# One row transfer an iteration from a ring, ranks in a rotating PSUM bank, and a reordered start

## The chip, the cores and the metric

The kernel runs on one NeuronCore of one Trainium2 chip. The core has four compute engines that run side by side, each through its own list of instructions in order: TensorE (PE in the profile; weight loads are PEld), VectorE (DVE), ScalarE (ACT) and GpSimd (POOL). SyncE (SP) only starts transfers. Transfers that SP starts and those that GpSimd starts use different queues on the same 16 DMA engines. The metric is the device time in microseconds (us) of one execution. The engines wait for each other through semaphores, which a framework places wherever one instruction needs what another leaves; the order within each engine is the order of the program text.

## The reference

Attention with a local window, then a dense MLP plus a mixture of eight experts with one expert a token:

```
B, H, S, D = 4, 8, 768, 64        # 3072 tokens, model width 512
for each chunk of 32 queries:
    keys, values = 8 memory rows + 16 left + 32 own + 8 right     # 64 rows
    a = softmax(q @ keys.T / 8);  attn = a @ values
x = attn as [3072, 512]
y = relu(x @ w1_dense) @ w2_dense
logits = x @ w_gate;  e = argmax;  gate = softmax(logits)[e]
y += gate * (relu(x @ w1[e]) @ w2[e])
```

All inputs and the output are float32; the large products run in bfloat16, the products that decide the gate in float32.

## The kernel before

There are two stages. The first goes over 24 tiles of 128 tokens (six a batch) and ends by scattering each tile's rows into a buffer `xs` in device memory, sorted by expert. The second fetches 31 slots of 128 rows from `xs`, multiplies each by its expert's weights and scatters the result to the output.

A row that is scattered has 770 words (`ROW`): x in bfloat16, the dense result in float32 (from `YD`), the gate weight (`GW`) and the token number (`GW + 1`). Rows are made in groups (`GROUPS`): seven groups of three tiles, then one of two and one of one. A group's rows lie in one tile `row` of a pool with two buffers.

**The loop (L481 to L532).** Iteration g works on several tiles at once: scores of tile g, the turning of the probabilities of g - 1, `values` of g - 2, `turn_x` of g - 3, and gate, dense1, dense2 of g - 4. There are 28 iterations. The program text gives each engine its order: gate and dense1, `turn_x`, scores, values, one key or query block of the next batch (`turn_qk`), turn, exp, dense2, perhaps another block, rank, ship.

- `values` (L278) leaves the attention output `xn` (one buffer). GpSimd casts it into `row` (L297).
- `turn_x` (L300) transposes `xn`; ScalarE copies it to `x32`, then VectorE casts it to `xT`, in this order.
- `gate` (L310) writes logits into the PSUM tile `pgt`. With the last tile of a group it calls `choose` (L357), which finds the expert and leaves `ex`, `oh`.
- `rank` (L383) counts, for a group, how many earlier tokens chose the same expert. Its matmuls write another part of the same tile `pgt`; VectorE reads it at L404 and leaves the row numbers `si` (L409). It also sums `ex` and writes the gate weights into the rows (L401, L402).
- `ship` (L413) starts the group's three scatters on GpSimd, one after the other (L416).
- `new_group` (L350) takes the next `row` buffer and copies the token numbers into it (L355).

PSUM tiles named `ps` rotate over three buffers: `xtp`, `sc`, `tp`, `ap` take them in turn, and each taker waits until the one three before has been read.

**Values.** The values of half a batch lie in one of three tiles `vw`: 64 rows a head, of which 8 are memory rows. `fill_v` (L154) writes the memory rows from `memv` over a whole block, `load_v` and `load_end` (L161, L179) then load the values over it, and `shift_v` (L189) copies the rows that two neighbouring chunks share. In the loop the fills run on GpSimd in every iteration with g % 3 = 1, and the shifts on VectorE and ScalarE in those with g % 3 = 0 and 1. A load of expert weights by GpSimd (L83) follows the ship from iteration 6 on.

**The start (L448 to L478).** Four pairs of key and query loads are started on GpSimd, then the first values, the memories and the gate weights on SP; VectorE clears both key tiles `kbd` and fills its half of `vw` 0; the memory keys `mk` follow the four pairs; ScalarE fills the other half. Then come constants, two more pairs, the dense weights, the fill of `vw` 1 on GpSimd, and the transposes of batch 0: eight steps through the `ps` buffers, emptied by ScalarE and VectorE (L224, L230). The key copies on VectorE wait for those on ScalarE.

GpSimd's transfers use eight semaphores in turn, and so do SP's: each transfer waits until the eighth before it has landed.

Of the kernel before, what the change touches and what calls it, by code (L numbers as in the profile page):

```python
# [38 lines left out]
GRP = 3  # L39
# [7 lines left out]
def kernel(  # L47
# [63 lines left out]
    with ExitStack() as one:  # L111
# [4 lines left out]
        rows = one.enter_context(tc.tile_pool(name="rows", bufs=2))  # L116
# [12 lines left out]
        memv = c1.tile([128, B * HP, D], F32, name="memv")  # L129
        wgate = c1.tile([128, DT, E], F32, name="wgate")  # L130
        mk = c1.tile([128, 128], BF16, name="mk")

        qk_todo = [(b, hp) for b in range(B) for hp in range(HP)]
        qk = {}
# [102 lines left out]
        def attention(g, qT, kbd):  # L237
# [40 lines left out]
            def values():  # L278
                vw = vws[g // 3 % NV]
                xp = px.tile([128, 2, 512], F32, tag="xp", name="xp")  # L280
                for hp in range(HP):
                    for par in range(2):
                        r = slice(64 * par, 64 * par + 64)
                        for cc in range(4):
                            nc.tensor.matmul(  # L285
                                xp[32 * cc:32 * cc + 32, par, (D + 1) * hp:(D + 1) * (hp + 1)],
                                st["aT"][r, hp, 32 * cc:32 * cc + 32],
                                vw[r, hp, 4 * (g % 3) + cc, :], start=True, stop=True,
                                tile_position=(64 * par, 32 * cc))
                xv = xp[:, :, :HP * (D + 1)].rearrange("p a (h d) -> p a h d", d=D + 1)  # L290
                rs = small.tile([128, 2, HP], F32, tag="rs", name="rs")
                nc.vector.reciprocal(rs, xv[:, :, :, D])
                xn = work.tile([128, DM], F32, tag="xn", name="xn")
                nc.vector.tensor_tensor(  # L294
                    xn.rearrange("p (h a d) -> p a h d", a=2, d=D), xv[:, :, :, :D],
                    rs.unsqueeze(3).to_broadcast([128, 2, HP, D]), ALU.mult)
                nc.gpsimd.tensor_copy(grp["row"][:, u, :YD].bitcast(BF16), xn)  # L297
                st["xn"] = xn

            def turn_x():  # L300
# [8 lines left out]

            def gate():  # L310
                for d in range(DT):
                    nc.tensor.matmul(grp["pg"][:, 0, u, :], st["x32"][:, d, :], wgate[:, d, :],  # L312
                                     start=(d == 0), stop=(d == DT - 1))
                if u == grp["size"] - 1:
                    choose(grp)
# [18 lines left out]
            def last(part):  # L334
                if u == grp["size"] - 1:
                    part(grp)

            return {"scores": scores, "exp": expo, "turn": turn, "values": values,
                    "turn_x": turn_x, "gate": gate, "dense1": dense1, "dense2": dense2,
                    "rank": lambda: last(rank), "ship": lambda: last(ship)}  # L340
# [7 lines left out]
        pgt = pg.tile([128, 3, 2, GRP, E], F32, name="pgt")  # L348

        def new_group(n):  # L350
            grp = grps[n]
            grp["row"] = rows.tile([128, GRP, ROW], F32, tag="row", name="row")
            grp["pg"] = pgt[:, n % 2]
            k, t = grp["size"], grp["first"]
            nc.gpsimd.tensor_copy(grp["row"][:, :k, GW + 1].bitcast(I32), tok[:, t:t + k])  # L355

        def choose(grp):  # L357
            k = grp["size"]
            SH = [128, k, E]

            def wide(ap):
                return ap.unsqueeze(2).to_broadcast(SH)

            def st(shape, name, dt=F32):
                return small.tile(shape, dt, tag=f"{name}{k}", name=name)

            lg = grp["pg"][:, 0, :k]
# [12 lines left out]
            nc.scalar.activation(ex, df, AF.Exp, bias=0.0, scale=1.0)  # L380
            grp["ex"], grp["oh"] = ex, oh

        def rank(grp):  # L383
            k = grp["size"]
            SH = [128, k, E]
            rk, row, ex, oh = grp["pg"][:, 1, :k], grp["row"], grp["ex"], grp["oh"]

            def st(shape, name, dt=F32):
                return small.tile(shape, dt, tag=f"{name}{k}", name=name)


# [8 lines left out]
            es = st([128, k], "es")  # L400
            nc.vector.reduce_sum(es, ex, axis=AX.X)  # L401
            nc.vector.reciprocal(row[:, :k, GW], es)  # L402
            at = st(SH, "at")
            nc.vector.tensor_tensor(at, rk, ecap.unsqueeze(1).to_broadcast(SH), ALU.add)  # L404
            nc.vector.tensor_tensor(at, at, oh, ALU.mult)
            sl = st([128, k], "sl")
            nc.vector.reduce_sum(sl, at, axis=AX.X)
            si = st([128, k], "si", I32)
            nc.vector.tensor_copy(si, sl)  # L409
            nc.vector.tensor_tensor(oh_sum[:, :k], oh_sum[:, :k], oh, ALU.add)  # L410
            grp["si"] = si

        def ship(grp):  # L413
            row, si = grp["row"], grp["si"]
            for t in range(grp["size"]):
                i = nc.gpsimd.indirect_dma_start(  # L416
                    xs[:, :], bass.IndirectOffsetOnAxis(ap=si[:, t:t + 1], axis=0),
                    row[:, t, :].bitcast(I32), None, bounds_check=E * SPAN - 1, oob_is_err=False)
                for o in scatters:
                    tc.declare_no_dep(i.ins, o.ins, reason="different rows of xs")  # L420
                scatters.append(i)


        thr_i = c1.tile([128, NT], I32, name="thr_i")
# [20 lines left out]
                nc.vector.memset(low[:, e, :e], 1.0)  # L445


        for _ in range(HP):  # L448
            load_qk()
        nc.vector.memset(memv, 0.0)  # L450
        for vw in vws:
            nc.vector.memset(vw[:, :, :, D:], 1.0)
        for par in range(2):
            nc.vector.memset(vws[0][64 * par:64 * par + 32, :, 0, :D], 0.0)
        load_v(0)
        load_memories()
        nc.sync.dma_start(wgate, moe_w_gate.rearrange("(t p) m -> p t m", p=128))
        for kb in kbds:
            nc.vector.memset(kb, 0.0)
        nc.vector.memset(mkbd, 0.0)  # L460
        load_mk()
        for par in range(2):
            fill_v(0, nc.scalar.copy if par else nc.vector.tensor_copy,
                   slice(64 * par + 32, 64 * par + 64))
        load_end(0)
        constants()
        table_constants()
        for _ in range(QKB - HP):
# [8 lines left out]
            s()  # L477
        mem_keys()  # L478
        steps = []
        ALL = slice(0, HP)  # L480
        for g in range(NT + 4):  # L481
            def do(part, lag):
                if 0 <= g - lag < NT:
# [51 lines left out]
        def tmp(shape, name, dt=F32):  # L535
            return small.tile(shape, dt, name=name, bufs=1)

        cp = pgt[:, 2, 0, 0]
# [185 lines left out]
```

## Time and profile before

| | us |
|---|---|
| median of the runs (309.37 to 314.36) | 309.46 |
| profiled execution | 309.23 |
| its span, first to last instruction | 307.5 |
| first scores on TensorE | 27.09 |
| last scatter to `xs` starts | 219.33 |
| first fetch of `xs` ends TensorE's wait | 227.83 |
| last output scatter starts | 299.52 |

TensorE is busy for 75% of the span, VectorE 62%, ScalarE 50%, GpSimd 45%; the mean granted TensorE clock is 0.904 of full speed. The DMA engines moved 54.1 MB.

The profile is read in this way. The chain of work that ended last goes back from the last instruction to whatever released each one. The table of waits adds up, for each line, how long its engine stood idle before it and which instruction ended that. A timeline lists instructions as "start, duration, engine, line, operation, output <- input", with the idle time before in brackets. A table of stretches gives the busy time of each engine (instructions in brackets), then the granted clock, the DMA share and GB/s. "Issue" is idle time for which the profile shows no cause.

### The profile page before, as it was taken

To read this page: it belongs to the slowest core of one execution; us is meant where nothing else is said; L and a number is where in the kernel's file an instruction comes from. 1 tells how busy PE (TensorE), PEld (TensorE's weight loads), DVE (VectorE), ACT (ScalarE), POOL (GpSimd) and SP (SyncE) were. 2 spreads that over 40 slices of the span, in tenths; PEclk is the share of its full clock that TensorE was granted. 3 is DMA by queue.
4 is the path that set the end of the run, shared out by engine and by line. 5 is a ranking of instruction groups with operands and counts; after the bars stand their busy time and mean duration, and the time that the engine had idled before them with its cause. 6 is when DMAs were issued, how large, how long until landed. Compare 5 with 4: busy or idle time off the path is not lost.

```text
span 307.5 us, 9871 instructions
## 1 busy us (share of the span) xinstructions
PE 231.3 (75%) x4028; PEld 182.3 (59%) x4063; DVE 190.8 (62%) x424; ACT 154.0 (50%) x240; POOL 138.8 (45%) x160
## 2 busy tenths in 40 slices
PE   0216788968888877978878788969229869999990
PEld 0115577756766765866766667858127547766760
DVE  6356666767768767768874744634824547776760
ACT  0085766755575664766754454523105435555540
POOL 9187634437457227327335032042202625556552
PEclk9999989997997997989986976995857999999996
DMA  7979999658999959957968915340373999998830
GB/s 125 186 98 181 191 205 131 110 129 167 187 192 212 156 95 206 166 122 179 179 124 176 272 63 205 104 156 13 143 230 112 233 344 306 320 317 294 288 117 0
DMA packets 56076, 54.10 MB, mean 176 GB/s; under 512 B 30558, under 2 KB 47966, under 8 KB 56032
## 3 DMA queue, kind: packets, MB, share of 16 engines
q0 software_dynamic: 22896, 31.53, 49.4%
q1 hardware_dynamic: 33136, 21.95, 29.9%
q8 instruction: 32, 0.52, 0.7%
q14 instruction: 12, 0.10, 0.1%
HBM read 50.31 MB, written 20.74 MB: 231 GB/s over the span
## 4 chain that ended last, share of the span: by engine, by line
PE 38%; issue 22%; POOL 12%; DVE 10%; ACT 6%; POOLq 1%; DVEq 0%; ACTq 0%
POOL out_dram L668 11%; PE xp L285 8%; PE ph L321 7%; PE pgt L312 7%; PE py L330 5%; PE ap L273 3%; PE xtp L303 3%; PE tp L219 3%; DVE vw L193 2%; PE sc L252 2%; DVE a L263 2%; DVE mx L261 2%; DVE xT L307 1%; ACT vw L193 1%; ACT x L305 1%
## 5 line engine op out<-in xcount | busy, mean ns | idle before, releaser
L668 POOL DMA_INDIRECT out_dram<-o,dest x31 | 35.8, 1155 | 44.0 <-DVE o L666 41.1
L297 POOL CAST row<-xn 128x512 bf16<-128x512 f32 x24 | 16.1, 669 | 79.2 <-DVE xn L294 79.2
L285 PE MATMUL xp<-vw,aT 64*32 64x65 f32 x1536 | 31.4, 239 | 15.1 <-issue 13.7
L307 DVE CAST xT<-xtp 128x512 bf16<-128x512 f32 x24 | 16.6, 692 | 37.9 <-ACT x L305 36.0
L645 PE MATMUL ph<-xT,wa 128*128 128x128 bf16 x496 | 34.4, 225 | 1.7 <-ACT xT L624 1.1
L285 PEld LDWEIGHTS xp<-vw,aT 64*32 64x32 f32 x1536 | 21.7, 112 | 23.3 <-issue 19.4
L666 DVE SCALAR_TENSOR_TENSOR o<-py,xg 128x512 f32<-128x512 f32 x31 | 23.3, 751 | 19.4 <-issue 10.0
L416 POOL DMA_INDIRECT xs<-row,si x24 | 24.4, 1016 | 23.0 <-DVE oh_sum L410 5.3
L312 PEld LDWEIGHTS pgt<-wgate,x 128*128 128x128 f32 x192 | 26.8, 208 | 13.3 <-ACT row L332 6.5
L312 PE MATMUL pgt<-wgate,x 128*128 128x8 f32 x192 | 26.4, 263 | 9.5 <-DVE at L404 8.1
L624 ACT COPY xT<-xt 128x512 bf16<-128x512 bf16 x31 | 18.1, 586 | 29.3 <-PE xt L622 21.0
L645 PEld LDWEIGHTS <-wa 128*128 128x128 bf16 x496 | 30.6, 101 | 2.4 <-issue 1.4
L658 PE MATMUL py<-wall,h 128*128 (+1 forms) x112 | 30.4, 381 | 1.8 <-ACT h L648 0.8
L321 PE MATMUL ph<-xT,wall 128*128 128x128 bf16 x384 | 28.5, 234 | 0.0
L635 DVE COPY wa<-wall 128x2048 bf16 (+1 forms) x31 | 21.5, 695 | 10.9 <-PE ph L645 5.2
L321 PEld LDWEIGHTS <-wall 128*128 128x128 bf16 x384 | 26.9, 111 | 0.0
L330 PE MATMUL py<-wall,h 128*128 128x512 bf16 x73 | 24.7, 455 | 2.8 <-issue 1.3
L648 ACT ACTIVATE h<-ph 128x512 bf16<-128x512 f32 x31 | 18.5, 597 | 14.0 <-PE ph L645 13.7
L193 DVE COPY vw<-vw 24x1408 f32<-24x1408 f32 (+1 forms) x15 | 25.2, 1679 | 0.5
L230 ACT COPY kbd<-tp 64x768 bf16<-64x768 bf16 x16 | 12.7, 792 | 25.5 <-PE tp L219 25.5
L275 ACT COPY aT<-ap 128x512 f32<-128x512 f32 x24 | 14.0, 584 | 19.9 <-PE ap L273 19.9
L622 PE MATMUL xt<-ident,xg 128*128 128x128 bf16 x124 | 12.5, 228 | 12.7 <-DMA xg<-xs 12.5
(113 smaller groups left out, 442.9 us busy)
## 6 DMA issues: line engine op xcount, KB each, us to landing
xg<-xs SPq DMA_DIRECT2D x31, 385.0 KB
wall<-in_moe_w_dram POOLq DMA_DIRECT2D x16, 512.0 KB
xs<-wall SPq DMA_DIRECT2D x8, 385.0 KB
kb<-in_k_dram POOLq DMA_DIRECT2D x16, 192.0 KB
qb<-in_q_dram POOLq DMA_DIRECT2D x16, 192.0 KB
vw<-in_v_dram SPq DMA_DIRECT2D x32, 96.0 KB
vw<-in_v_dram SPq DMA_DIRECT2D x32, 88.0 KB
wall<-in_moe_w_dense_dram POOLq DMA_DIRECT2D x2, 512.0 KB
```

The lines of the kernel that those rows point to most:

```text
L193: copy(vw[r + 32:r + CTX, hps, :VC - 1, :D], vw[r:r + CTX - 32, hps, 1:, :D])
L285: nc.tensor.matmul(xp[32 * cc:32 * cc + 32, par, (D + 1) * hp:(D + 1) * (hp + 1)], st["aT"][r, hp, 32 * cc:32 * cc + 32], vw[r, hp, 4 * (g ...
L307: nc.vector.tensor_copy(xT, xtp)
L312: nc.tensor.matmul(grp["pg"][:, 0, u, :], st["x32"][:, d, :], wgate[:, d, :], start=(d == 0), stop=(d == DT - 1))
L321: nc.tensor.matmul(ph[:, f, :], wall[:, E, d, 128 * f:128 * f + 128], st["xT"][:, d, :], start=(d == 0), stop=(d == DT - 1))
L330: nc.tensor.matmul(py, st["h"][:, f, :], wall[:, E, DT + f, :], start=(f == 0), stop=(f == FT - 1))
L416: i = nc.gpsimd.indirect_dma_start(xs[:, :], bass.IndirectOffsetOnAxis(ap=si[:, t:t + 1], axis=0), row[:, t, :].bitcast(I32), None, bounds ...
L635: nc.vector.tensor_copy(wa, wall[:, :min(j + 1, E)][:, bass.ds(low_enough(of_dve[j], j), 1), :DT] .rearrange("p a t m -> p (a t) m"))
L645: nc.tensor.matmul(ph[:, f, :], wa[:, d, 128 * f:128 * f + 128], xT[:, d, :], start=(d == 0), stop=(d == DT - 1))
L658: nc.tensor.matmul(py, h[:, f, :], wall[:, :min(j + 1, E)][:, bass.ds(e, 1), DT + f] .rearrange("p a m -> p (a m)"), start=(f == 0), stop= ...
L666: nc.vector.scalar_tensor_tensor(o, py, xg[:, GW:GW + 1], xg[:, YD:GW], op0=ALU.mult, op1=ALU.add)
L668: i = nc.gpsimd.indirect_dma_start(out[:, :], bass.IndirectOffsetOnAxis(ap=dest[:, j:j + 1], axis=0), o, None, bounds_check=NT * 128 - 1, ...
```

## The change

Five things change together.

1. **Ring.** The two `row` buffers become one tile `ring` of six rows; tile t uses place t % 6. The token number is copied for each tile behind its cast instead of once a group.
2. **Ship.** `rank` appends its tiles to a list `ready`, and each iteration starts one scatter from it, before the weight load. The last iterations empty the list.
3. **Rank.** The rank's matmuls write a `ps` tile named `rk` instead of a part of `pgt`. The sum of `ex` and its reciprocal move from `rank` to `choose`.
4. **Start.** The memories are the first transfers of SP; the memory keys follow the second pair of loads; the second key tile `kbd` is cleared in iteration 0 instead of the start; `fill_v(0)` and `load_end(0)` come right behind the first values; the fill of `vw` 1 comes before two pairs of loads and the dense weights.
5. **First shift.** The shift of `vw` 0 for one lane half is done in the start by GpSimd; that for the other half is split between VectorE and ScalarE in iteration 0, where before each of the two engines did one whole half.

```diff
+        ring = c1.tile([128, 2 * GRP, ROW], F32, name="ring")
...
                 nc.gpsimd.tensor_copy(grp["row"][:, u, :YD].bitcast(BF16), xn)
+                nc.gpsimd.tensor_copy(grp["row"][:, u, GW + 1:].bitcast(I32), tok[:, g:g + 1])
...
-            grp["row"] = rows.tile([128, GRP, ROW], F32, tag="row", name="row")
+            grp["row"] = ring[:, t % (2 * GRP):t % (2 * GRP) + k]
             grp["pg"] = pgt[:, n % 2]
-            nc.gpsimd.tensor_copy(grp["row"][:, :k, GW + 1].bitcast(I32), tok[:, t:t + k])
...
             nc.scalar.activation(ex, df, AF.Exp, bias=0.0, scale=1.0)
-            grp["ex"], grp["oh"] = ex, oh
+            es = st([128, k], "es")
+            nc.vector.reduce_sum(es, ex, axis=AX.X)
+            nc.vector.reciprocal(grp["row"][:, :k, GW], es)
+            grp["oh"] = oh
...
-            rk, row, ex, oh = grp["pg"][:, 1, :k], grp["row"], grp["ex"], grp["oh"]
+            oh = grp["oh"]
+            rk = ps.tile([128, k, E], F32, tag="ps", name="rk")
...
-        def ship(grp):
-            row, si = grp["row"], grp["si"]
-            for t in range(grp["size"]):
-                i = nc.gpsimd.indirect_dma_start(
-                    xs[:, :], bass.IndirectOffsetOnAxis(ap=si[:, t:t + 1], axis=0),
-                    row[:, t, :].bitcast(I32), None, bounds_check=E * SPAN - 1, oob_is_err=False)
...
+            ready.extend((grp, t) for t in range(k))
+        ready = []
+        def ship():
+            if not ready:
+                return
+            grp, t = ready.pop(0)
+            i = nc.gpsimd.indirect_dma_start(
+                xs[:, :], bass.IndirectOffsetOnAxis(ap=grp["si"][:, t:t + 1], axis=0),
+                grp["row"][:, t, :].bitcast(I32), None, bounds_check=E * SPAN - 1, oob_is_err=False)
...
-        for _ in range(HP):
-            load_qk()
         nc.vector.memset(memv, 0.0)
+        load_memories()
+        load_qk()
+        load_qk()
+        load_mk()
+        load_qk()
+        load_qk()
...
         load_v(0)
-        load_memories()
+        nc.vector.memset(kbds[0], 0.0)
+        fill_v(0, nc.scalar.copy, slice(32, 64))
+        fill_v(0, nc.vector.tensor_copy, slice(96, 128))
+        load_end(0)
         nc.sync.dma_start(wgate, moe_w_gate.rearrange("(t p) m -> p t m", p=128))
-        for kb in kbds:
-            nc.vector.memset(kb, 0.0)
         nc.vector.memset(mkbd, 0.0)
-        load_mk()
-        for par in range(2):
-            fill_v(0, nc.scalar.copy if par else nc.vector.tensor_copy,
-                   slice(64 * par + 32, 64 * par + 64))
-        load_end(0)
         constants()
         table_constants()
+        fill_v(1, nc.gpsimd.tensor_copy, slice(0, 128))
         for _ in range(QKB - HP):
             load_qk()
         load_w(2)
-        fill_v(1, nc.gpsimd.tensor_copy, slice(0, 128))
+        shift_v(0, 0, slice(0, HP), nc.gpsimd.tensor_copy)
...
-            do("ship", 4)
+            ship()
+            if g >= NT + 2:
+                while ready:
+                    ship()
             if g == 0:
-                shift_v(0, 0, ALL, nc.vector.tensor_copy)
-                shift_v(0, 1, ALL, nc.scalar.copy)
+                nc.vector.memset(kbds[1], 0.0)
+                shift_v(0, 1, slice(0, 2), nc.vector.tensor_copy)
+                shift_v(0, 1, slice(2, 4), nc.scalar.copy)
```

More of the change, by code (lines that the diff above doesn't have):

```diff
@@ L115 @@
         work = one.enter_context(tc.tile_pool(name="work", bufs=1))
-        rows = one.enter_context(tc.tile_pool(name="rows", bufs=2))
         small = one.enter_context(tc.tile_pool(name="small", bufs=2))
@@ L311, in gate @@
                 for d in range(DT):
-                    nc.tensor.matmul(grp["pg"][:, 0, u, :], st["x32"][:, d, :], wgate[:, d, :],
+                    nc.tensor.matmul(grp["pg"][:, u, :], st["x32"][:, d, :], wgate[:, d, :],
                                      start=(d == 0), stop=(d == DT - 1))
@@ L339, in attention @@
                     "turn_x": turn_x, "gate": gate, "dense1": dense1, "dense2": dense2,
-                    "rank": lambda: last(rank), "ship": lambda: last(ship)}
+                    "rank": lambda: last(rank)}
         scatters = []
@@ L347 @@
             of_tile += [n] * size
-        pgt = pg.tile([128, 3, 2, GRP, E], F32, name="pgt")
+        pgt = pg.tile([128, 3, GRP, E], F32, name="pgt")
         def new_group(n):
             grp = grps[n]
-            grp["row"] = rows.tile([128, GRP, ROW], F32, tag="row", name="row")
+            k, t = grp["size"], grp["first"]
+            grp["row"] = ring[:, t % (2 * GRP):t % (2 * GRP) + k]
             grp["pg"] = pgt[:, n % 2]
-            k, t = grp["size"], grp["first"]
-            nc.gpsimd.tensor_copy(grp["row"][:, :k, GW + 1].bitcast(I32), tok[:, t:t + k])
         def choose(grp):
@@ L365, in st @@
                 return small.tile(shape, dt, tag=f"{name}{k}", name=name)
-            lg = grp["pg"][:, 0, :k]
+            lg = grp["pg"][:, :k]
             mx = st([128, k], "gmx")
@@ L399, in rank @@
                                  start=False, stop=(t == k - 2))
-            es = st([128, k], "es")
-            nc.vector.reduce_sum(es, ex, axis=AX.X)
-            nc.vector.reciprocal(row[:, :k, GW], es)
             at = st(SH, "at")
@@ L411, in rank @@
             grp["si"] = si
-        def ship(grp):
-            row, si = grp["row"], grp["si"]
-            for t in range(grp["size"]):
-                i = nc.gpsimd.indirect_dma_start(
-                    xs[:, :], bass.IndirectOffsetOnAxis(ap=si[:, t:t + 1], axis=0),
-                    row[:, t, :].bitcast(I32), None, bounds_check=E * SPAN - 1, oob_is_err=False)
-                for o in scatters:
-                    tc.declare_no_dep(i.ins, o.ins, reason="different rows of xs")
-                scatters.append(i)
+            ready.extend((grp, t) for t in range(k))
[7 more added lines that the diff above has]
+                grp["row"][:, t, :].bitcast(I32), None, bounds_check=E * SPAN - 1, oob_is_err=False)
+            for o in scatters:
+                tc.declare_no_dep(i.ins, o.ins, reason="different rows of xs")
+            scatters.append(i)
         thr_i = c1.tile([128, NT], I32, name="thr_i")
@@ L479 @@
         steps = []
-        ALL = slice(0, HP)
         for g in range(NT + 4):
@@ L536, in tmp @@
             return small.tile(shape, dt, name=name, bufs=1)
-        cp = pgt[:, 2, 0, 0]
+        cp = pgt[:, 2, 0]
         for t in range(GRP):
```

## The prediction

> **What bounds the kernel now.** I read the page's chain first, then the waits, then the timelines of the places they name. The chain's shares (page, part 4):
>
> ```profile
> PE 38%; issue 22%; POOL 12%; DVE 10%; ACT 6%; POOLq 1%; DVEq 0%; ACTq 0%
> ```
>
> No engine carries it: the chain changes engine at nearly every link, so the loop of 28 iterations is bound by hand-overs between engines. The POOL share is the second stage (236 to 300 us), where the change touches nothing. There are three places to look at. The table of waits (engine, line, waited for: us in total, times, longest) names two:
>
> ```profile
> ACT L158 <- DMA memv<-in_mem_v_dram: 15.9, 1, 15.9
> PE xp L285 <- issue: 13.7, 28, 1.8
> PE pgt L312 <- DVE at L404: 8.1, 6, 1.9
> ```
>
> The first is the start. ScalarE's first work in program order is its half of `fill_v(0)`, and it sits on the memories until 15.89. Its timeline (start us, us):
>
> ```profile
> 15.89 1.28 ACT L158 ACT_TABLE_LOAD   x1 [15.89 <-DMA memv<-in_mem_v_dram]
> 17.19 2.75 ACT L158 COPY vw<-memv 32x3072 f32<-32x3072 f32 x1
> 19.96 0.79 ACT L230 COPY kbd<-tp 64x768 bf16<-64x768 bf16 x1
> ...
> 25.82 0.80 ACT L224 COPY qT<-tp 128x768 bf16<-128x768 bf16 x1 [0.25 <-PE tp L219]
> ```
>
> Three transposes had been done by 11 us; TensorE then stood for 10.5 us, because all three `ps` buffers were full and the engine that empties them was waiting. The first scores follow at 27.09. The load of data was over long before, as the stretches show (last two columns: DMA share, GB/s):
>
> ```profile
> 14.00:16.00 2.00, 0.00 (x0) 0.00 (x0) 1.45 (x1) 0.11 (x1) 0.00 (x0) 1.00 1.14 130
> 16.00:18.00 2.00, 0.00 (x0) 0.00 (x0) 1.47 (x34) 1.99 (x2) 1.37 (x6) 1.00 0.13 17
> ```
>
> The share is 0.71 to 1.39 from 2 to 16 us and falls to 0.13 after; by the DMA records the fourth query load ends at 16.3. So about 10 us of the start are order, not bandwidth.
>
> The second place is the end of each group of three. On TensorE (timeline; brackets give the idle time before):
>
> ```profile
> 64.73 1.03 PE L312 MATMUL pgt<-wgate,x 128*128 128x8 f32 x8 [1.91 <-DVE at L404]
> ...
> 68.42 0.34 PE L285 MATMUL xp<-vw,aT 64*32 64x65 f32 x6 [0.42 <-issue]
> 69.19 0.33 PE L285 MATMUL xp<-vw,aT 64*32 64x65 f32 x6 [0.43 <-issue]
> 69.95 0.32 PE L285 MATMUL xp<-vw,aT 64*32 64x65 f32 x4 [0.43 <-issue]
> ```
>
> Gate and rank share the tile `pgt`, so the next gate stands until VectorE has read the rank. The holes in `xp` without a cause come while the three scatters run (POOL L416 at 66.34, 67.73, 69.07). In all seven groups whose scatters meet `xp`, holes of 0.3 to 0.5 us lie from about 1.65 us after the first scatter's start to 0.7 us after the last one's end: 25 of them, about 10.4 us, and they are on the chain. Why they come I cannot say.
>
> The third is the shared work of VectorE and GpSimd:
>
> ```profile
> 96.44 0.81 POOL L83 DMA_DIRECT2D wall<-in_moe_w_dram  x1
> 96.83 3.93 DVE L193 COPY vw<-vw 24x1408 f32<-24x1408 f32 x1
> 97.24 2.77 POOL L158 COPY vw<-memv 128x3072 f32<-128x3072 f32 x1
> ```
>
> The same copy takes 0.89 at 165.16. Four of them (74.08, 96.83, 120.81, 143.65) end 0.76 us after the POOL fill that runs beside them.
>
> **The change part by part.** The profiled run took 309.23 us (span 307.5 plus 1.7 around it), 0.1% under the median of 309.46; sums are made against 309.23.
>
> *Start.* The memories go first on SP, behind the 0.91 us memset of `memv` (done at 2.02), so they should land near 4.5 instead of 14.5. ScalarE: table load 1.28 + fill 2.75 ends near 8.6. From there the data sets the pace. Ahead of the last query load lie the same eight loads, now with the memory keys in the middle, and key and value packets share the DMA engines as they did; I take 17 us for 16.3. Behind it: transposes 0.85, `qT` 0.80, `mkbd` 0.46, and about 1 us of queueing on the three buffers: scores near 20.1, 7.0 earlier. Bounds: 8.5 earlier if nothing queues, 3 if VectorE's first `kbd` copies stand behind the POOL fill that now runs inside the start (2.76 us a copy). What follows must also be early: the next key load needs to be there at 21 and is fourth-query time plus 1.4, 18.4; dense weights landed at 31.7 and are needed from 44.05, now 37; POOL stood until 32.53 for those weights, then filled (2.76) and cast row 0 at 37.02. That chain moves perhaps 2 to 3 us only, to 34, while `xn` of tile 1 needs that cast done at 41.18 - 6.2 = 35. It fits with 1 us to spare. Given back: the second `kbd` memset (2.70) moves in front of tile 1's `mx` on VectorE, while VectorE's shift there halves from 1.62 to 0.95 (the other lane block went to POOL, in the start, behind the value loads): 2.0 later on VectorE. Beside it ScalarE's shift shrinks from 2.54 to 1.37, but its `kbd` copy now waits for the memset, 0.5 earlier than before in all. `aT` is on the path first, then the scores: I charge 0.8. **Start: -6.2.**
>
> *Rank in a rotating bank.* The gate no longer waits: 1.91, 0.58, 1.81, 1.66, 1.80 and 0.36 = 8.1 us go. What is late next? At 64.73: a gate at 62.83 has `ph` done by 64.8; ScalarE is busy to 65.84 with `row` and the shift, so `h` starts at 65.84 instead of 66.77, and `xT` follows. Of 1.9 us 0.93 pass. So 4 x 0.9 + 2 x 0.3 = **-4.2** (bounds 0 and -8.1). The extra `ps` tile sends `xtp` to wait for `aT`, whose copy ends 2 us or more before; nothing. The sum and reciprocal move from rank to choose, 2 x 0.18, behind an `ex` that ends (59.92) before `oh` does (60.31); nothing.
>
> *One scatter an iteration.* Same 24 scatters. The burst of three goes, and with one scatter 1.65 after the start and 0.7 after the end nearly close the window. But every iteration now has one, and some fall on `xp`. Between all 10.4 gone and all kept, at the middle: **-5**. The 24 token copies (0.19 for three before) follow the cast on POOL, in front of the scatter: off the path. The ring gives each row two iterations from scatter to rewriting, as the two row tiles did; rows landed 2.9 to 5.3 us after the issue in the groups I looked at, and an iteration takes 5.2 to 10: no wait. The end is as it was: tile 20's scatter stands ahead of rank 7, and the last one still waits for the last dense row (219.33).
>
> *Scatter in front of weight load and fill.* In four iterations POOL now runs cast, scatter (1.06), weight load, fill, where it ran cast, weight load, fill. The shift on VectorE starts 0.95 to 1.5 after the cast starts, that is inside the scatter. If POOL's DMA work holds it off, as the row at 96.83 says (0.41 into the weight load's span and still behind the fill), it ends 1.35 later than now. `xT` there starts with ScalarE's `x` today (77.79 against a shift that ends at 77.45), so 0.9 shows: 4 x 0.9 = **+3.6**. If it slips in ahead of the fill it shows nothing, since ScalarE is as late: 0. The two copies beside key loads (43.66 and 51.32, 0.95 instead of 0.89) speak for this end. The nearer row is 96.83, the same three POOL instructions: I take +3.6.
>
> [...]
>
> Sum: -6.2 - 4.2 - 5.0 + 3.6 = -11.8, so **297.4**. TensorE's granted clock (0.95, 0.92, 0.93, 0.93, 0.80 over stretches of the loop) may move 3 us either way.
>
> **Rivals.**
> - *Only the start counts, 303* (chance 0.20): single scatters make as many holes, one or two in each iteration, and the lock gives back the gate's gain: 309.2 - 6.2. For it: 22% of issue is spread widely. Against: no holes in most iterations without scatters.
> - *All of it, 289* (0.14): no holes (-10.4), shifts slip in ahead of the fill (0): -6.2 - 4.2 - 10.4 = -20.8, 288.4. The short iterations of the loop (5.2 us between casts against 8 to 9.8) show there is room.
> - *The start is not what it says, 306* (0.10): the keys were the limit after all, or TensorE now waits 3 us later for what comes behind them (-3 instead of -6.2, the loop at 0). For it: 0.9 and more of DMA share from 18 to 50 us.
> - *Slower, 317* (0.08): the single `xn` buffer. A row's cast waits for the scatter of six tiles before; that scatter now stands behind a weight load each time (4 to 6 us by the records), and TensorE's next `xn` waits for the cast. One such wait exists:
>
> ```profile
> 210.28 0.19 POOL L355 COPY row<-tok 128x1 int32<-128x1 int32 x1 [4.41 <-DMA xs<-row,si]
> ```
>
>   It decides once a scatter lands over two iterations, some 13 us, after its issue. At 1.1 us in each of 18 rewrites it costs 20: 309.2 - 11.8 + 20 = 317.
>
> **How the numbers follow.** 0.48 for the forecast. Faster by over 2% (under 303.3; 2% is about what measurement can tell from no change): most of the forecast, the 289, half of the 303, 0.72. Within 2%: 0.20. Slower: 0.08. The range 288 to 306 takes in the unknown costs (holes -10.4 to 0, lock 0 to 3.6, start -8.5 to -3) and leaves the slower case out.
>
> **What would show it.** Right: ScalarE's fill by 9 us and first scores near 20; no gate wait on VectorE; fewer holes in `xp`, none in rows of four; L193 still 3 us and more in four iterations and ending with the fill. Wrong: scores after 24; holes in every iteration; long waits of POOL's cast on `xs`; more throttling as TensorE fills up.

## The result

| | before | after |
|---|---|---|
| median of the runs on one chip, us (range) | 309.41 (307.48 to 314.36) | 280.71 (277.92 to 289.99) |
| ratio, 95% interval | | 0.9045 [0.8951, 0.9139] |
| profiled execution, us | 309.23 | 280.06 |
| first scores on TensorE | 27.09 | 20.30 |
| `xn` of tile 2 to `xn` of tile 22 (the loop) | 150.1 | 126.0 |
| of these at half TensorE clock | 30.7 | 6.8 |
| `xn` of tile 22 to tile 23 | 7.7 | 9.1 |

The kernel is faster by 28.7 us where 11.8 were forecast, and the time lies below the range. Some executions of a kernel take 1.6% and more above its fastest, mostly at a lower granted clock (w5: 0.878 to 0.913 against 0.925): ratios leave them out, medians do not, and the traces of x1, x5, x7, x10, x11, w2, w5, w10 and w11 below are of such executions, so that sums from them are rough. The start brings what was worked out; the loop brings 24 us (150.1 less 126.0) where the sum had 5.6. The half-clock time is added up from the records of the granted clock. The chain's shares of the kernel after can't be set against those of before:

```profile
PE 13%; DMA 7%; issue 6%; POOL 1%; POOLq 0%; DVE 0%; DVEq 0%
```

They add up to 27% of the span: this time the chain could be followed back only that far, into the second stage. The readings below go by timelines and waits.

**The start.** ScalarE's timeline of the kernel after, in the same columns as before:

```profile
4.32 1.28 ACT L158 ACT_TABLE_LOAD   x1 [4.32 <-DMA memv<-in_mem_v_dram]
5.62 2.75 ACT L158 COPY vw<-memv 32x3072 f32<-32x3072 f32 x1
8.39 0.79 ACT L230 COPY kbd<-tp 64x768 bf16<-64x768 bf16 x1
...
19.41 0.80 ACT L224 COPY qT<-tp 128x768 bf16<-128x768 bf16 x1 [0.63 <-PE tp L219]
```

The fill ends at 8.37 (forecast: 8.6), and the wait for the memories is 4.3 instead of 15.9.

**Gate, holes and shift.** TensorE's timeline of the kernel after, at a group's end:

```profile
68.35 0.95 PE L313 MATMUL pgt<-wgate,x 128*128 128x8 f32 x8
69.16 1.05 PE L322 MATMUL ph<-xT,wall 128*128 128x128 bf16 x16
...
70.98 0.86 PE L285 MATMUL xp<-vw,aT 64*32 64x65 f32 x64
```

The gate has no idle time before it, and 64 matmuls of `xp` run through in 0.86 us. Where a scatter falls on `xp` a hole is sometimes left, here beside a scatter at 99.69:

```profile
99.43 0.66 PE L285 MATMUL xp<-vw,aT 64*32 64x65 f32 x41
100.25 0.30 PE L285 MATMUL xp<-vw,aT 64*32 64x65 f32 x4 [0.16 <-issue]
101.01 0.47 PE L285 MATMUL xp<-vw,aT 64*32 64x65 f32 x19 [0.45 <-issue]
```

Holes of 0.15 to 0.45 us add up to 2.3 us in the loop, where before there were 25 with 10.2 us. And the shift L193, which was to stay at 3 us and more in four iterations and to end with the fill, takes 0.88 to 0.89 in all of them from 59 us on. The timelines of GpSimd, then of VectorE, after:

```profile
63.56 0.61 POOL L297 CAST ring<-xn 128x512 bf16<-128x512 f32 x1 [1.73 <-DVE xn L294]
64.12 0.18 POOL L298 COPY ring<-tok 128x1 int32<-128x1 int32 x1
64.47 1.08 POOL L423 DMA_INDIRECT xs<-ring,si  x1 [0.16 <-POOL ring L298]
65.54 0.77 POOL L83 DMA_DIRECT2D wall<-in_moe_w_dram  x1
66.29 2.77 POOL L158 COPY vw<-memv 128x3072 f32<-128x3072 f32 x1
...
64.52 0.89 DVE L193 COPY vw<-vw 24x1408 f32<-24x1408 f32 x1
66.25 0.69 DVE L308 CAST xT<-xtp 128x512 bf16<-128x512 f32 x1 [0.84 <-ACT x L306]
```

The scatter's 1.08 us stand where the shift runs: it starts 0.05 after the scatter and ends 0.88 before the fill begins. The work in front of the fill delays the fill and not the shift.

**A new wait.** From the table of waits of the kernel after (engine, line, waited for: us, times, longest):

```profile
POOL xs L423 <- DMA xs<-wall: 9.2, 1, 9.2
...
PE xp L285 <- issue: 4.8, 10, 1.3
...
DVE xn L294 <- POOL ring L297: 4.6, 1, 4.6
...
ACT L158 <- DMA memv<-in_mem_v_dram: 4.3, 1, 4.3
```

A scatter waits 9.2 us for the pad rows that SP writes from `wall` into `xs` (L541); GpSimd's cast stands behind it, and VectorE's `xn` of tile 23, which needs the one `xn` buffer, behind the cast. This is the step from tile 22 to 23 in the table. Nothing of it was in the sum.

### The profile page after: what moved, and what is told of

Read it like the earlier page. It is cut to its first block, busy times and chain, and to the rows that moved or that the text cites. A ratio compares the mean times of both kernels' runs of the same rounds, so it can differ in the third digit from the quotient of the medians.

```text
span 278.4 us, 9898 instructions
## 1 busy us (share of the span) xinstructions
PE 215.4 (77%) x4028; PEld 170.6 (61%) x4063; DVE 181.8 (65%) x424; ACT 152.4 (55%) x240; POOL 142.1 (51%) x176
## 5 line engine op out<-in xcount | busy, mean ns | idle before, releaser
L297 POOL CAST ring<-xn 128x512 bf16<-128x512 f32 x24 | 15.4, 642 | 50.5 <-DVE xn L294 49.7
L423 POOL DMA_INDIRECT xs<-ring,si x24 | 25.2, 1049 | 30.1 <-DMA xs<-wall 9.2
L285 PE MATMUL xp<-vw,aT 64*32 64x65 f32 x1536 | 25.5, 236 | 5.6 <-issue 4.8
L322 PE MATMUL ph<-xT,wall 128*128 128x128 bf16 x384 | 25.8, 221 | 1.8 <-issue 1.8
L313 PEld LDWEIGHTS pgt<-wgate,x 128*128 128x128 f32 x192 | 24.9, 197 | 2.5 <-issue 0.6
L331 PE MATMUL py<-wall,h 128*128 128x512 bf16 x73 | 22.1, 414 | 5.1 <-ACT h L325 2.8
L285 PEld LDWEIGHTS xp<-vw,aT 64*32 64x32 f32 x1536 | 19.2, 110 | 10.2 <-issue 7.4
L322 PEld LDWEIGHTS <-wall 128*128 128x128 bf16 x384 | 24.2, 104 | 1.8 <-issue 1.8
L633 PE MATMUL xt<-ident,xg 128*128 128x128 bf16 x124 | 12.5, 228 | 12.8 <-DMA xg<-xs 12.3
L633 PEld LDWEIGHTS <-xg 128*128 128x128 bf16 x124 | 9.2, 102 | 21.3 <-issue 11.9
L294 DVE TENSOR_TENSOR xn<-xp,rs 128x512 f32<-128x512 f32 x24 | 16.6, 692 | 7.0 <-POOL ring L297 4.6
```

The costliest lines, as they stand in the source:

```text
L285: nc.tensor.matmul(xp[32 * cc:32 * cc + 32, par, (D + 1) * hp:(D + 1) * (hp + 1)], st["aT"][r, hp, 32 * cc:32 * cc + 32], vw[r, hp, 4 * (g ...
L313: nc.tensor.matmul(grp["pg"][:, u, :], st["x32"][:, d, :], wgate[:, d, :], start=(d == 0), stop=(d == DT - 1))
L322: nc.tensor.matmul(ph[:, f, :], wall[:, E, d, 128 * f:128 * f + 128], st["xT"][:, d, :], start=(d == 0), stop=(d == DT - 1))
L331: nc.tensor.matmul(py, st["h"][:, f, :], wall[:, E, DT + f, :], start=(f == 0), stop=(f == FT - 1))
L423: i = nc.gpsimd.indirect_dma_start(xs[:, :], bass.IndirectOffsetOnAxis(ap=grp["si"][:, t:t + 1], axis=0), grp["row"][:, t, :].bitcast(I32) ...
L633: nc.tensor.transpose(xt[:, d, :], xb[:, 128 * d:128 * d + 128], ident)
```

## The experiments

Eighteen runs followed, of ten changed kernels and of the two above, on chips numbered 7, 11, 12 and 13. The kernel before takes 294 to 295 us on 7 and 12, and 308 to 311 on 11 and 13, as it did at the record; so each ratio below is against the kernel before on the same chip, with its 95% interval.

### Each part alone (chip 12)

`x1_start`: the kernel before with the new order of the start and the new first shift.

> The kernel before with the new start alone (order of loads, fills and memsets, first shift). Both theories have the same for it. The recorded sum: scores near 20 instead of 27.1, total about 303 (-6.2, bounds -8.5 and -3). The rival, that the loop of the changed kernel got its 21 us because an early start changes what meets what later (loads, weight transfers, the clock): more than 10 us gone, under 299.

288.63 against 294.29, ratio 0.9787 [0.9606, 0.9969]: 5.7 us by the medians, 1 to 12 by the interval. First scores come at 19.94.

`x2_bank`: the kernel before with the rank in a `ps` tile and the sum of `ex` in `choose`.

```diff
-            rk, row, ex, oh = grp["pg"][:, 1, :k], grp["row"], grp["ex"], grp["oh"]
+            oh = grp["oh"]
+            rk = ps.tile([128, k, E], F32, tag="ps", name="rk")
...
```

> The kernel before with the rank in a rotating bank and the gate weight made in choose, nothing else. Recorded sum: -4.2, about 305, the gate's wait on VectorE's rank gone (8.1 us). If the holes in the 64 small matmuls of xp belong to the three scatters, all 25 stay, since the burst stays. If they came from the rank's order they go and it is -10 or more.

Slower, by 0.5 to 4%: 1.0216 [1.0053, 1.0378]. The gate's wait is gone. In its place TensorE waits for the shift, as GpSimd, VectorE and TensorE show one after the other in x2's timelines:

```profile
71.72 0.65 POOL L297 CAST row<-xn 128x512 bf16<-128x512 f32 x1
72.28 0.82 POOL L83 DMA_DIRECT2D wall<-in_moe_w_dram  x1
73.07 2.78 POOL L158 COPY vw<-memv 128x3072 f32<-128x3072 f32 x1
...
71.79 4.82 DVE L193 COPY vw<-vw 24x1408 f32<-24x1408 f32 x1
...
76.66 0.64 PE L285 MATMUL xp<-vw,aT 64*32 64x65 f32 x26 [3.77 <-DVE vw L193]
```

The shift comes up earlier, here 1.28 us ahead of the fill, 0.41 at 96.83 in the kernel before at the record, and it ends where it ended there, 0.76 us behind the fill (76.61 against 75.85). Four such waits make 13.7 us, 8.3 in the kernel before on chip 7.

`x3_ring`: the kernel before with the ring and one scatter an iteration.

```diff
...
-            do("ship", 4)
+            ship()
...
```

> The kernel before with the ring and one scatter an iteration alone. Recorded sum: holes -5, lock +3.6, so about 308, with the shift copy of 3.4 to 3.9 us in four iterations and ending with the fill. New theory, from the trace of the changed kernel: the scatter delays the fill past the shift, all shifts take 0.89, holes fall from 10.4 to under 5, and both together give -12 to -16, about 295.

1.0103 [0.9917, 1.0289]; the 12 to 16 us that were expected did not come. From 60 us on all shifts take 0.88 to 0.89 us, but the gate's wait stays (7.2 us, five times) and the pad wait comes (9.3). From `xn` of tile 2 to that of 22 it takes 133.9 us, where the kernel before on chip 7 takes 134.6; the step to tile 23 grows from 5.3 there to 10.4.

`x4_fill`: the kernel before with load and fill of the values one iteration later; scatters stay in threes.

```diff
-            n = (g + 5) // 3
-            if g % 3 == 1 and n < 2 * B:
+            n = (g + 4) // 3
+            if g % 3 == 2 and n < 2 * B:
```

> The kernel before with the fill and load of a value block one iteration later, where there is no shift; nothing else. Recorded working: a shift that is held up shows nothing, since ScalarE is as late: 309, no change. New theory: the four collisions cost about 2 us each, -6 to -10, about 301, while the holes in xp stay at about 10 us. If the value loads come too late for their shift, it is slower than that.

0.9966 [0.9866, 1.0065]; the 6 to 10 us that were expected did not come either. The shifts take 0.9 to 1.1; the gate's wait is 11.2 us, 8.5 in the kernel before on chip 7. So the gate's wait and the held-off shift lie over each other, in part: set beside the kernel before on chip 7, 5.4 of the gate's 8.5 us come back as wait for the shift in x2, and 2.7 of the shift's 8.3 as wait for the gate in x4. The rest goes otherwise: into the pad wait in x3, and with half clock in x2 and x4 (20.5 and 23.9 us of the loop, 10.2 in the kernel before on chip 7).

### The shift against the fill, with the gate's wait gone (chip 7, and 12 again)

`y_before` and `y_after` are the two kernels once more.

> The kernel before again, unchanged, for a trace from the chip of this call: the last call had 294.3 us for it where the first trace comes from an execution of 309.2. If the 0.42 us holes in xp and the half-clock stretches (10.4 us and 41 us of the loop in the first trace) belong to the program they are here too; if they belong to that chip they are not, and then they explain the 15 us.

> The changed kernel again, unchanged, beside the others on one chip. If its gain is the program's: ratio near 0.90. If 15 us of the 29 were that chip's holes and clock, met by the burst of scatters: ratio near 0.95, that is the start (-6) and the shifts (-8) alone.

After: 277.60 against 293.98, ratio 0.96 [0.9527, 0.9673]. The kernel after is about as fast here as at the record (280.71); it is the kernel before that is 15 us faster. Its trace shows why in part: the scatters fall on `xp` as before, and there are no holes. TensorE, then GpSimd, of the kernel before on chip 7:

```profile
111.84 1.18 PE L285 MATMUL xp<-vw,aT 64*32 64x65 f32 x64
...
110.65 1.06 POOL L416 DMA_INDIRECT xs<-row,si  x1 [1.34 <-ACT vw L193]
112.01 1.03 POOL L416 DMA_INDIRECT xs<-row,si  x1 [0.30 <-ACT h L324]
```

`x5_burst`: the kernel after with its scatters in threes.

```diff
-            ship()
-            if g >= NT + 2:
-                while ready:
-                    ship()
+            while ready:
+                ship()
```

> The changed kernel with a group's three scatters started together again, in the iteration of the rank; all else as changed. In the iterations of the fill POOL then runs cast, token copy, weight load, fill without a scatter between. Recorded working: +5 (the holes come back), shifts end 1.35 earlier (-3.6): about +1. New theory: the shifts run into the fill again in four iterations (3.4 to 4.8 us instead of 0.89): +8 to +14, and on a chip with holes more.

0.986 [0.9814, 0.9906], by the ratios 7.5 us more than the kernel after. Shifts of 4.7 to 5.1, and 14.0 us of TensorE's waits for them; no rows of holes in `xp`.

`x6_fillfirst` and `w6_fillfirst`: the kernel after, in which the scatter comes behind weight load and fill in iterations with g % 3 == 1. Single scatters stay, only the order on GpSimd is the old one.

```diff
-            ship()
+            if g % 3 != 1 or g >= NT:
+                ship()
...
             if g % 3 == 1 and n < 2 * B:
...
                 load_v(n)
                 load_end(n)
+            if g % 3 == 1 and g < NT:
+                ship()
```

> The changed kernel with one scatter an iteration, but in the iterations with a fill (g % 3 = 1) the scatter comes behind the fill on GpSimd instead of in front of the weight load. Recorded working: the shift ends 1.35 earlier: -3.6 or 0. New theory: the four shifts run into the fill again: +8 to +12 over the changed kernel, with no burst and so with no holes. If x5_burst is slower than this one, the rest is the burst.

> The changed kernel with the scatter behind the fill once more: single scatters, collision kept. Theory (each of collision and bursts costs by itself where the other is gone): shifts L193 of 4.0 us in four iterations; ratio 0.935 to 0.95 where the kernel before takes 308 to 311 us (the changed kernel 0.905 to 0.915 there, and 9 us more), 0.99 where it takes about 292. Rival (with single scatters the collision is hidden where there are holes): 0.905 to 0.92 on the first sort of chip.

0.9939 [0.9818, 1.0061] on chip 7 and 0.9814 [0.9775, 0.9852] on chip 12, shifts of 4.0: on chip 7, 9.0 us more than the kernel after; the kernel after was not run on chip 12, where 0.99 had been expected. The wait itself is 10.6 us over four shifts in w6; behind it there can be a second cost. The stretches of w6, each wait's 3.4 us and the 10.2 behind it (us, busy time of PE, PEld, DVE, ACT, POOL, then granted clock, DMA share, GB/s):

```profile
66.20:69.60 3.40, 1.08 (x32) 0.78 (x30) 3.40 (x1) 1.64 (x3) 3.23 (x2) 1.00 1.10 160
69.60:79.80 10.20, 9.56 (x148) 7.99 (x156) 4.65 (x14) 4.00 (x7) 5.46 (x7) 0.50 1.08 215
90.40:93.80 3.40, 1.78 (x45) 1.49 (x42) 3.38 (x1) 2.39 (x3) 3.26 (x2) 1.00 1.06 163
93.80:104.00 10.20, 9.53 (x232) 7.87 (x233) 8.76 (x22) 5.80 (x11) 4.12 (x5) 1.00 1.09 213
```

Where TensorE stood 2.96 us, its clock is halved for 10.2 us and it gets through 148 matmuls; where it stood 2.29, the clock stays and it gets through 232. The iteration after the first wait takes 9.5 us from `xn` to `xn`, the one after the second 6.3. The length alone does not decide. In the eight runs with such waits (x1, x2, x5, x6, w2, w5, w6, y_before), all eight waits for the shift of 3.0 us and more come with stretches at half clock that begin near their end (3.4 to 10.2 us); of fifteen between 2.3 and 3.0, eight do (up to 13.7 us). The stretches at half clock come in steps of 3.41 us (3.41, 6.83 and 13.65 in the kernel before at the record). After the first wait above the clock came back after three steps, and in the 3.40 us ahead of the half clock TensorE was at work for 1.08.

In the traces of the kernels before and after at the record, all stretches at half clock begin on a grid of 3.41 us (before: 43.46, 70.77, 94.66, 118.55, 135.62 and on). Those of w6 fit one too (from 69.6 above to 114.0, where another begins, it is 13 steps). Of its first wait, 67.28 to 70.24, 2.32 us lie in a single step, 66.20 to 69.60 above; the second, 92.18 to 94.47, is split between two, 1.32 and 0.97, which TensorE fills to more than half each (same columns):

```profile
90.09:93.50 3.41, 2.09 (x49) 1.80 (x49) 3.38 (x2) 2.67 (x4) 3.41 (x3) 1.00 1.02 156
93.50:96.92 3.42, 2.45 (x76) 1.77 (x76) 3.22 (x6) 1.15 (x2) 1.68 (x2) 1.00 1.20 217
```

In the traces of the kernels before and after at the record there are 72 steps at full clock from 40 us to `xn` of tile 22. TensorE was busy for 47 to 66% of 14 of them, and ten of these were followed by half clock; it was busy for 71% and more of the other 58, and none was. What decides within the 14 is not shown.

### Bank and ring without the start, and the pads (chip 11)

`z_after`: the kernel after once more.

> The changed kernel again, as the measure for the three others on the same chip. Two earlier chips gave ratios of 0.9045 and 0.96 to the kernel before. Theory (the long gain belongs to the chip on which the kernel before takes 309 us): 0.96 here if the kernel before takes 289 to 294 us, 0.905 if it takes 309.

281.38 against 308.38, 0.9145 [0.9083, 0.9206].

`x9_bank_ring`: x2 and x3 together, with the old start.

> The kernel before with the rank bank and the ring with one scatter an iteration, the start left as it was. Theory (the gate's wait and the held-off shift hide each other, so that each alone brings nothing and both together do): shifts L193 of 0.9 us in all iterations, no gate wait, xn of tile 22 about 10 us earlier than in the kernel before, some 5 of them given back at the pad wait: ratio 0.98 (0.97 to 0.99). Rival (the two edits are independent): the product of their single ratios, 1.02 times 1.01, so 1.01 to 1.03; then the gain of the changed kernel would need the new start.

0.9347 [0.9291, 0.9403]: 19.7 us under the kernel before, and 7.3 over the kernel after, which is what the start is worth. The loop takes 123.4 us, none of it at half clock, with shifts of 0.9, no gate wait, and two single holes of 0.43 us in place of the record's 25. Bank and ring are not independent. The gain is three times the expected one; that holes went too on this chip fits, but bank and ring without the start were not run on a chip without holes.

`x7_pads`: the kernel after, with pad writes and scatters declared independent, since they write different rows of `xs`.

```diff
-                    nc.sync.dma_start(
+                    i = nc.sync.dma_start(
...
+                    for o in scatters:
+                        tc.declare_no_dep(i.ins, o.ins, reason="different rows of xs")
+                    pads.append(i)
...
-            for o in scatters:
+            for o in scatters + pads:
```

> The changed kernel with the pad rows' writes and the scatters declared independent of each other (they touch different rows of xs). Theory (the scatter at tile 20 stands 9 us behind the pad writes, POOL's cast behind it, and xn of tile 23 behind that, 9 to 10 us after xn of tile 22 instead of about 4.6): the wait of xs on wall goes, the gap falls to about 5, and the time is 4 to 6 us below the changed kernel. Rival (the last dense rows or the second stage hide it anyway): the gap falls, the time stays within 1 us.

276.44, 0.8926 [0.8868, 0.8985]: 4.9 us under the kernel after on the same chip, and the fastest of all. `xn` of tile 23 comes 5.1 us after that of 22 instead of 9.6, and the wait of `xs` for `wall` is not in the table.

### The bursts of three (chips 11, 13 and 12)

`x10_bank_fill` and `w10_bank_fill`: the bank, and the fill one iteration later as in x4; old start, row tiles, scatters in threes. `w2_bank` is x2 once more.

> The kernel before with the rank bank and the value load and fill one iteration later; bursts of three scatters and the two row tiles stay. It takes the collision away without ring or single scatters. Theory (it is the fill on POOL against the shift on VectorE that counts, not how the scatters lie): shifts of about 0.9 to 1.1 us, no gate wait, no pad wait: ratio 0.965 (0.955 to 0.98), lower than that of bank and ring. Rival (single scatters are what pays): 1.00 to 1.02, as with the bank alone.

> Bank and later fill, bursts kept, once more. Theory (the held-off shift costs 9 to 14 us on any chip once the gate's wait is gone): 0.03 to 0.05 of the ratio below the bank alone on this chip, with or without holes in xp. Rival (the shift is hidden, the bursts are what costs): within 0.01 of the bank alone.

> The bank alone once more, as the measure for the next kernel on the same chip. Both theories: no gate wait, shifts L193 of 4.5 to 5.2 us in four iterations, ratio 1.00 to 1.03.

The theory fell. On chip 11 x10 gives 0.9777 [0.9711, 0.9844], within its range but far above bank and ring on the same chip (0.9347), where it was to lie below. On chip 13 the bank alone gives 0.9609 [0.9525, 0.9693], a gain where it had been a loss, with shifts of 3.2 to 3.9 us; with the shift freed it is 0.9738 [0.9643, 0.9832], no better. In w10 TensorE waits 0.4 us for the shift, and 9.3 us of "issue" lie before `xp` (w2: 5.0 and 9.9). The holes are about as many in both (18 and 16); in w10 two of the groups run at 67.5 to 72.3 and 91.7 to 96.6, 4.8 us for 64 matmuls. Where the 4.6 us of the shift's wait go in w10, these two traces do not tell.

`w5_burst` is x5 on chip 13; `x11_burst_fill` and `w11_burst_fill` are x5 with the later fill of x4.

> The changed kernel with its scatters together in threes, once more. Both theories: shifts L193 of 4.7 to 5.1 us in four iterations; ratio 0.975 to 0.99. Holes of about 0.42 us in xp where the kernel before takes 308 us on this chip, none where it takes about 290.

> The changed kernel with its scatters in threes and the value load and fill one iteration later, so that no fill runs beside a shift. Theory: shifts of 0.9 to 1.1 us, no gate wait, no pad wait; 0.03 to 0.05 of the ratio below the scatters in threes alone; on a chip without holes about 0.945, below the changed kernel's 0.96 by the pad wait that it lacks; on a chip with holes about 0.955, above the changed kernel's 0.905 to 0.9145. Rival (the bursts cost the same on every chip, holes or not): above the changed kernel by 0.03 and more everywhere.

> The changed kernel with scatters in threes and the fill one iteration later, once more: bursts kept, collision gone. Theory (bursts cost only by the holes that they leave): 0.952 again where the kernel before takes 308 to 311 us; where it takes about 292 no holes, and 0.945 to 0.96, no more than the changed kernel's 0.96. Rival (bursts cost without holes too): 0.98 and more on the second sort of chip.

Chip 13: w5 300.06 against 310.78 by medians, 0.966 (its five runs, 292.86 to 305.67, give no interval), with shifts of 3.4 to 4.0 us instead of 4.7 to 5.1 and 20 holes of 0.25 to 0.44 from 83 us on; x11 0.9521 [0.9428, 0.9615]. Chip 12: w11 0.9502 [0.943, 0.9575]. TensorE and GpSimd of x11 on chip 13, then TensorE and GpSimd of w11 on chip 12:

```profile
198.65 0.68 PE L285 MATMUL xp<-vw,aT 64*32 64x65 f32 x42
199.77 0.34 PE L285 MATMUL xp<-vw,aT 64*32 64x65 f32 x6 [0.44 <-issue]
200.54 0.31 PE L285 MATMUL xp<-vw,aT 64*32 64x65 f32 x5 [0.43 <-issue]
...
198.47 0.98 POOL L423 DMA_INDIRECT xs<-ring,si  x1 [1.18 <-issue]
199.76 0.98 POOL L423 DMA_INDIRECT xs<-ring,si  x1 [0.30 <-ACT x L306]
```

```profile
167.29 0.86 PE L285 MATMUL xp<-vw,aT 64*32 64x65 f32 x64
...
165.33 1.06 POOL L423 DMA_INDIRECT xs<-ring,si  x1 [3.39 <-DMA xs<-wall]
166.69 1.03 POOL L423 DMA_INDIRECT xs<-ring,si  x1 [0.30 <-ACT h L325]
168.03 0.98 POOL L423 DMA_INDIRECT xs<-ring,si  x1 [0.30 <-issue]
```

The same program, the same meeting of `xp` and burst; on one chip holes of 0.43, on the other none. Where there are none, scatters in threes cost little once the shift is free: 0.9502 is no worse than the kernel after (0.96 on chip 7), which has a pad wait of about 9 us where w11 has 3.4. A cost of the size of that difference is not excluded. Where there are holes, they do cost: x10 against x9 on chip 11, 0.9777 against 0.9347 with the old start; and 0.9521 for x11 on chip 13 against 0.9145 and 0.9045 for the kernel after on other chips.

## Why the prediction was wrong, step by step

- **Start, -6.2: right.** First scores at 20.30 (forecast 20.1). Alone 5.7 us on chip 12 (interval 1 to 12); 7.3 between x9 and the kernel after on chip 11.
- **Rank bank, -4.2: right on the wait, wrong on what is late next.** All gate waits go. The sum let ScalarE's `h` be next. What is next is the shift on VectorE: in x2 TensorE waits 13.7 us for it, and the bank alone loses 2% on chip 12. In the record's profile TensorE's own wait for L193 was 0.7 us, where the kernel before on chip 7, without holes, has 8.3 with the same gate's wait: by this comparison the holes came first; it could not be read from the table, only by asking what the shift would do if everything before it came earlier. On chip 13 the bank alone gains 12.1 us; where that comes from its trace does not tell.
- **Lock, +3.6: wrong in sign, and the main failure.** The lock of the sum is the step with the scatter in front of weight load and fill, where GpSimd was to hold the shift off. No run shows a scatter that does so; in its place, with single scatters all shifts take 0.88 to 0.89 us (x3 and the kernel after, from 60 us on). "The nearer row is 96.83, the same three POOL instructions", said the step. They are the same, but with a scatter between cast and weight load the shift is done before the fill starts. The row at 96.83 shows a shift beside weight load and fill; it says nothing of a shift beside a scatter. The rows at 43.66 and 51.32 show one inside GpSimd's DMA work that lost only 0.06, the second of them 1.10 ahead of a fill, and were set aside as the farther ones. With the gate's wait gone the scatter in front of the fill is worth 9.0 us (x6 against y_after), where a loss of 3.6 was charged: four waits of 2.3 to 3 us are saved, and half clock behind some of them. On chip 7 the forecast for gate and lock together, with no holes to lose, is -0.6; the loop gets 11.3 us shorter there (134.55 to 123.21). This is shown on the chips without holes; with single scatters it was not run on one with holes.
- **Holes, -5: right in kind, too small.** At the record 10.2 us became 2.3, so 7.9 went. On chips 12 and 7 there were none to remove.
- **Clock, 3 us either way: too narrow, and taken for a thing apart.** Half-clock time in the loop fell from 30.7 to 6.8 us. It is in part a consequence of the waits, as the eight waits of 3.0 us and more show. How much of the 24 us it is can't be told; on chip 7 the loop gains its 11.3 us with 10.2 us of half clock before and 6.8 after, so there it can be little.
- **The pad wait was not seen:** 4.9 us given back (x7). It has the shape of the rival "slower", a scatter that holds the cast and with it `xn`, but once and for another reason. The trace of before had the pad writes and their order; the step that moved each scatter past the iterations where they are issued did not ask about them.
- The forecast added its parts. Gate, shift and holes lie over each other, in part, at a group's end: on chips without holes neither gate nor shift pays alone (x2, x3, x4), and both do, with the new start (w11 and the kernel after); on chips with holes, gate and shift together pay little until the bursts go as well (x10 against x9). Set beside chip 7, 11.3 of the 24.1 us of the loop need no holes; the other 12.8 go with the holes and the half clock of the record's chip, in shares that no run tells apart. "All of it, 289" was the nearest case, 14% of the chance, and still 8 us too high.

## What to carry to other kernels

When several waits meet at one place of a loop, cost them together: take each away in thought, shift everything behind it, and ask which of the others then ends last; an edit that is worth nothing alone may be what another one needs. An instruction put between a GpSimd cast and a long GpSimd fill can be a gain if it gives a VectorE copy its time before the fill (9.0 us here, x6 against `y_after`). And a stand of TensorE of 3 us and more came with half clock in all eight cases here, so the longest waits are to be shortened first.

## What was not expected of the hardware

The same program takes 308 to 311 us at the record and on chips 11 and 13, and 294 to 295 on chips 7 and 12. One difference between them is seen where bursts of indirect scatters meet small fp32 matmuls: holes of mostly 0.41 to 0.44 us, one for every five or six matmuls, in rows on the first sort; on the second there are no rows, only single ones in a few traces. At half clock most are 0.28 to 0.33 us, and the step from one hole to the next is 0.7 to 0.8 us at either clock. Half clock differs too: 30.7 us of the loop at the record, 10.2 on chip 7. The profile gives the holes no cause ("issue"), and why chips differ stays open; the kernel after, which has no bursts in the loop, takes 277.6 to 281.4 on chips of either sort.

A VectorE copy beside GpSimd's scatter (kernel after: 64.52 in 64.47 to 65.55, 0.89) is not held up at all, while one that starts 0.50 ahead of the fill, inside a weight load, is held until 0.75 behind the fill's end. GpSimd, then VectorE, of w6:

```profile
65.91 0.77 POOL L83 DMA_DIRECT2D wall<-in_moe_w_dram  x1
66.67 2.76 POOL L158 COPY vw<-memv 128x3072 f32<-128x3072 f32 x1
...
66.17 4.01 DVE L193 COPY vw<-vw 24x1408 f32<-24x1408 f32 x1
```

The copy's record starts first here, and the copy ends behind the fill all the same. In x4 the copy starts 0.39 into a weight load, as it does at 96.83 in the kernel before at the record (3.93 us), but no fill follows:

```profile
75.06 0.80 POOL L83 DMA_DIRECT2D wall<-in_moe_w_dram  x1
...
75.45 1.10 DVE L193 COPY vw<-vw 24x1408 f32<-24x1408 f32 x1
```

So the weight load alone costs the copy 0.2 us (1.10 against 0.89), and the rest comes with the fill; why a copy that started before the fill ends behind it stays open.
